# Attention and a feed-forward layer on one core: new figures for the SyncE queue, the loads and a chunk's pace in the table that orders the program

## The chip, the core and the metric

The kernel runs on 1 of the 8 cores of a Trainium2 chip. The metric is the device time of one execution in microseconds (us). Five instruction queues work side by side: TensorE (PE, with its weight loads listed as PEld), VectorE (DVE), ScalarE (ACT), GpSimd (POOL) and SyncE (SP). In this kernel SP issues nearly all DMA transfers. Each queue executes in its written order: an instruction whose input is late also holds everything behind it on its engine.

## The reference

Inputs are q, k and v of 8 batches, 8 heads, 576 positions and 64 dimensions in fp32. Per batch two attentions are added:

- **pooled**: q, k and v are averaged over groups of 4 positions (576 becomes 144), softmax attention runs over all 144, and each output row is repeated 4 times;
- **local**: each position attends to the positions less than 4 away.

The sum, as 8 x 576 = 4608 rows of 512, is the `x` of a feed-forward layer with a residual:

```python
mu = np.mean(x, axis=-1, keepdims=True)
var = np.mean((x - mu) ** 2, axis=-1, keepdims=True)
xn = (x - mu) / np.sqrt(var + 1e-06) * g_ln
ch = np.maximum(xn @ w_ch1, 0.0) @ w_ch2      # 512 -> 2048 -> 512
return (x + ch).astype(np.float32)
```

The two weight matrices arrive as 64-bit floats.

## The kernel before

**Work.** The 4608 rows are 36 tiles of 128 rows and 18 chunks of 256 rows. The feed-forward part runs per chunk over 8 pairs of 128 hidden columns. Each matrix product is done as three fp32r products of high and low parts: `up` (L996, 12 matmuls per 128 columns) makes `h`, ACT makes `hh` (L1003) and DVE its rest `hl` (L1007), and `down` (L1019, 6 matmuls) adds into `acc`. The local attention of a batch is cut into 5 windows of 116 rows, 40 windows in all (`local(i)`); the pooled attention goes by half batches (`pooled_half`). For each tile, `norm(n)` adds both attentions (`plus`, L896, POOL), takes mean and variance (`stats`, L904 to L907, DVE), scales (`normed`, L914, DVE, makes `xn`), transposes on PE (L923, makes `px`) and splits into `xh` (ACT, L930) and `xlo` (DVE, L940).

**Windows.** Windows 0 to 6 load q and k by rows (L428, tiles `qn`, `kn`) and transpose them on PE (L458, `lq`, `lk`); later ones load 32-wide blocks (L419, `qr`, `kr`) and transpose on DVE (L499, `lqt`, `lkt`). L437 and L443 load `vwin`. The exponentials are transposed on PE (L575) and copied by ACT (L582, `at`), multiplied with `vwin` on PE (L596, `lv`) and divided by DVE (L602 to L612) into `xl`. The rows of `xl` are moved by DMA from one SBUF place to another, into the tile `x` (L653 to L662); the first tiles are instead put together on PE (`expand`, L884 and L890, `ex`).

**Weights.** `weights(which, f)` is called 32 times, for 16 groups of 128 hidden columns of each matrix: two loads of 256 KB (L347 or L352, tile `s`), ACT takes the high word (L359, `cva`), DVE joins the low word (L367, L370), ACT makes the high part (L378, `hi`), and DVE or POOL the low part (L383, `lo`). All of this has to happen during about the first eighth of the run, while the first chunks already use the weights.

**What sets the order.** No instruction's place is written by hand. Every piece of work is a task: `add(engine, duration, function, dependencies, due, take, give, lag, ahead, alt, kb)`. `Plan.order` fills the engines' queues in a modelled time: among the tasks that can start soonest on an engine (within 0.5 us) it takes the one that is due first. `lag` is how long after its end a task's result can be used; for loads with `kb`, a running sum `moved` at `rate` KB per us puts the landing later when much is in flight. A load is not started more than `ahead` before its due time. `take` and `give` count rooms: 88 buffers of 2 KB per partition (`u`), which most tiles share, 8 PSUM banks (`a`) and 2 staging buffers (`stg`). A buffer that a window's `xl` held is given back when the last of its moves has landed. The due times follow the chunks: chunk c is due at 35 + 55 c, and the windows, the pooled halves and the weights are placed from that. The result is only an order; what waits for what on the chip is settled by semaphores. Where the plan sees PE idle in its first part, it lets PE multiply the identity matrix (L197), whose result nobody uses.

Of the kernel before, what the change touches and what calls it, by code (L numbers as in the profile page):

```python
# [22 lines left out]
class Plan:  # L23
# [3 lines left out]
    def __init__(self, rooms, spare):  # L27


        self.tasks = []  # L30
        self.rooms = rooms
        self.spare = spare
        self.cold = 3
        self.hold = 0.5
        self.lags = (80, 0.3, 0.6)
        self.rate, self.moved = 245.0, 0.0

    def add(self, eng, dur, fn, deps=(), due=0.0, take=(), give=(), lag=None, ahead=1e9, alt=None, kb=0):

        opts = {eng: (dur, fn, 0.0)}  # L40
        if alt is not None:
            opts[alt[0]] = alt[1:]
        t = SimpleNamespace(
            n=len(self.tasks), opts=opts, dur=dur, deps=[d for d in deps if d is not None],
            due=due, take=take, give=give, lag=lag, ahead=ahead, open=0.0, waits=0, eng=None, fn=None, kb=kb,
        )
        self.tasks.append(t)
        return t
# [91 lines left out]
def attention_then_ffn(  # L140
# [129 lines left out]

    T0 = 35
    C1 = 5
    CHUNK = 55
    PACE = CHUNK / NPR

    def chunk_at(c):
# [40 lines left out]
        return tuple(n.items())  # L317

    U, A, STG = (("u", 1),), (("a", 1),), (("stg", 1),)
    DMA, LAT, W_AHEAD = 0.5, 2.9, 40  # L320

    def act(n, sbuf=False):
        return (0.155 if sbuf else 0.14) + n / 1430.0
# [13 lines left out]
    def weights(which, f):  # L337
        key = (which, f)
        name = f"{which}_{f}"
        due = W0 + W_GAP * (f // 2) + 0.5 * (which - 1) + 1.0 * (f % 2)  # L340

        def load():
            x = box[key] = SimpleNamespace()
            x.raw = [unit([P, 512], f"s{name}_{i}", I32) for i in range(2)]
            for i in range(2):
                if which == 1:
                    nc.sync.dma_start(  # L347
                        x.raw[i].rearrange("p (c e) -> p c e", c=KC // 2),
                        w1[256 * i : 256 * (i + 1), f * 2 * P : (f + 1) * 2 * P].rearrange("(c p) e -> p c e", p=P),
                    )  # L350
                else:
                    nc.sync.dma_start(x.raw[i], w2[f * P : (f + 1) * P, 512 * i : 512 * (i + 1)])  # L352

        def high_word():

            x = box[key]
            x.a = unit([P, 512], f"cva{name}", I32)
            for i in range(2):
                nc.scalar.activation(  # L359
                    x.a[:, 256 * i : 256 * (i + 1)].bitcast(F32),  # L360
                    x.raw[i].rearrange("p (n two) -> p n two", two=2)[:, :, 1].bitcast(F32),
                    AF.Prelu, scale=REBIAS, alpha=-(2.0**32),
                )

        def low_word():
            x = box[key]
            nc.vector.tensor_single_scalar(out=x.a, in_=x.a, scalar=3, op=ALU.logical_shift_left)  # L367
            for i in range(2):
                a = x.a[:, 256 * i : 256 * (i + 1)]
                nc.vector.scalar_tensor_tensor(  # L370
                    out=a, in0=x.raw[i].rearrange("p (n two) -> p n two", two=2)[:, :, 0], scalar=29, in1=a,
                    op0=ALU.logical_shift_right, op1=ALU.bitwise_or,
                )

        def high():
            x = box[key]
            x.hi = unit([P, 512], f"hi{name}", F32R)
            nc.scalar.copy(x.hi, x.a.bitcast(F32))  # L378

        def low(eng):  # L380
            x = box[key]
            lo = unit([P, 512], f"lo{name}", F32R)
            eng.tensor_sub(lo, x.a.bitcast(F32), x.hi.bitcast(F32))  # L383
            weight[key] = (x.hi, lo)

        add = plan.add
        t = add("SP", 2 * DMA, load, (), due, take=(("u", 3),), lag=LAT, kb=512, ahead=W_AHEAD)
        t = add("ACT", 2 * act(256, True), high_word, (t,), due)
        t = add("DVE", 0.45 + 2 * dve(256), low_word, (t,), due, give=(("u", 2),))
        t = add("ACT", act(512, True), high, (t,), due, take=U)  # L390
        return add("DVE", dve(512), lambda: low(nc.vector), (t,), due, take=U, give=U,
                   alt=("POOL", pool(512), lambda: low(nc.gpsimd), 0.3))
# [12 lines left out]
    def local(i):  # L405
# [45 lines left out]
        for src, nm in ((q, "q"), (k, "k")):  # L451
            if by_pe:

                def turn(nm=nm):
                    p = psa(f"l{nm}{i}")
                    x.p[nm] = p
                    for pr in range(NPAIR):
                        nc.tensor.transpose(  # L458
                            p[:, pr * P : (pr + 1) * P],
                            x.raw[nm][:, 2 * pr : 2 * pr + 2].rearrange("p h d -> p (h d)"), ident,  # L460
                        )

                def turn_out(nm=nm):
                    t = unit([P, NPAIR, P], f"l{nm}t{i}")
                    nc.scalar.copy(t.rearrange("p c t -> p (c t)"), x.p[nm])
                    setattr(x, nm + "t", t)

                def sums(nm=nm):

                    for par in range(2):  # L470
                        t0 = window_start(w, par)
                        g0, g1 = (-(-(NQ * (2 * w + p)) // FACTOR) for p in (par, par + 1))
                        g1 = min(g1, SD)
                        c0 = 64 * par + FACTOR * g0 - t0
                        p = x.p[nm].rearrange("p (c t) -> p c t", c=NPAIR)
                        for hg in range(2):
                            key = (b, hg, nm)
                            if key not in gsum:
                                gsum[key] = unit([P, 2, SD], f"gs{nm}{b}_{hg}")
                            nc.vector.tensor_reduce(  # L480
                                out=gsum[key][:, :, g0:g1],
                                in_=p[:, 2 * hg : 2 * hg + 2, c0 : c0 + FACTOR * (g1 - g0)]
                                .rearrange("p c (g r) -> p c g r", r=FACTOR),
                                axis=AX.X, op=ALU.add,
                            )

                t = add("SP", 1.46, lambda src=src, nm=nm: load_rows(src, nm), (), due - 12.0, take=U,
                        lag=LAT, kb=256, ahead=AHEAD)
                t = add("PE", 0.43, turn, (t,), due - 8.0, take=A, give=U)
                if own:  # L490
                    t = add("DVE", 4 * dve(120), sums, [t] + gsum_done.get((b, nm), []), due - 8.0,
                            take=() if w else (("u", 2),))
                    gsum_done.setdefault((b, nm), []).append(t)
                turned.append(add("ACT", act(512), turn_out, (t,), due - 8.0, take=U, give=A))
            else:

                def turn(nm=nm):
                    t = unit([P, H, 64], f"l{nm}t{i}")
                    nc.vector.transpose(  # L499
                        t.rearrange("p h j -> p (h j)"), x.raw[nm].rearrange("p h j d -> p (h j d)")  # L500
                    )
                    setattr(x, nm + "t", t)

                ts = []
                for jb in range(2):
                    ts.append(add("SP", 4 * DMA, lambda src=src, nm=nm, jb=jb: load_blocks(src, nm, jb), ts,
                                  due - 14.0, take=() if jb else U, lag=LAT, kb=128, ahead=AHEAD))
                turned.append(add("DVE", dve(512), turn, ts, due - 8.0, take=U, give=U))
        vt = add("SP", 4 * DMA, load_v, (last_local.v[i % NVW],), due - 8.0, lag=LAT, kb=256, ahead=AHEAD)

        def scores_by_pair():

# [138 lines left out]
        for e, (n, p0, r0, m, par) in enumerate(moves):  # L651

            def move(n=n, p0=p0, r0=r0, m=m, par=par):  # L653
# [7 lines left out]
                for h2 in range(2):  # L661
# [2 lines left out]
                        x.xl[64 * h2 + r0 : 64 * h2 + r0 + m].rearrange("p (c n) d -> p n c d", n=2)[:, par],  # L664
                    )

            t = add("SP", DMA if by_pe else 2 * DMA, move, outs, due + 1.0, take=() if n in piece else U,
                    give=U if e == len(moves) - 1 else (), lag=LAT, kb=116)
            piece.setdefault(n, []).append(t)

# [11 lines left out]
    def pooled_half(b, hg):  # L682
# [8 lines left out]
        for nm, src in (("v", v),) if own else (("q", q), ("k", k), ("v", v)):  # L691
            for half in range(2):
# [21 lines left out]
                    eng.tensor_add(dst[:, half, :, :D], raw[:, :, :D], raw[:, :, D : 2 * D])  # L714

                by_dve = b == 0 and nm == "k"
                t = add("SP", 0.82, load, (), due - 4.0, take=STG, lag=LAT, kb=288, ahead=AHEAD)
                t = add(
                    "DVE" if by_dve else "POOL", dve(512) + dve(256) if by_dve else 2.1,
                    (lambda key=key: pool4(key, nc.vector)) if by_dve else pool4, [t, lastg.vd[hg] if nm == "v" else None] + ready.get(nm, []),  # L720
# [6 lines left out]
    def pooled_pair(b, hg, pr, x, ready):  # L727
# [119 lines left out]
        lastg.v = lastg.vd[hg] = t  # L847
        t = add("DVE", 0.68, divided, (t,), due, take=U if b < NPB and pr == 0 else (), give=A)
        od_done.append(t)
        t = add("SP", DMA, keep, (t,), due, lag=LAT)  # L850
        ud_done.setdefault(b, []).append(t)


# [2 lines left out]
    def norm(n):  # L856
# [103 lines left out]
                    piece.setdefault(n1, []).append(m1)  # L960
            kept = add("ACT", act(512), keep_x, (t,), due + 1.0, take=U)
        else:
            t = add("SP", DMA * len(rows), load_up, [d for _, _, b, _ in rows for d in ud_done[b]], due - 4.0,
                    take=U, lag=LAT, kb=256, ahead=12.0)
            t = add("POOL", pool(512), plus, [t] + piece[n], due - 3.0, give=U)
        t = add("DVE", 1.1, stats, (t,), due - 1.0)
# [149 lines left out]
```

## Time and profile before

| | before |
|---|---|
| median of 3 runs | 1068.04 us (1065.08 to 1068.09) |
| profiled execution, its own time | 1069.35 us |
| span of its instructions | 1067.0 us |
| PE busy | 1039.3 us, 97% |
| DVE busy | 509.5 us, 48% |
| ACT busy | 313.2 us, 29% |
| POOL busy | 268.7 us, 25% |
| granted TensorE clock | 0.990 in the mean |
| moved by DMA | 104.33 MB in 289,295 packets, 237,945 of them under 512 B |

The execution's own time is 2.35 us over its span. PE is busy nearly all the time, so its gaps are what can be lost or won; they are few, and they lie in the first 140 us and at two places later. In a list of waits, "A <- B" reads: A waited, and what came last was B. In a chain, each row is the work or the transfer that released the next. In the table by stages each engine's busy time is followed by its number of instructions, and the granted clock, the share of the DMA engines and GB/s stand at the end.

### The profile page before, as it was taken

The numbers are of one execution on the slowest core, as the hardware profiler recorded it, in microseconds if no ns is written. First come the engines' busy times: TensorE is split into PE (matmuls) and PEld (weight loads), VectorE is DVE, ScalarE is ACT, GpSimd is POOL, SyncE is SP. The second block draws the span as 40 slices with busy tenths as digits, with TensorE's granted clock in tenths as the row PEclk, the third lists the DMA queues.
The fourth block names the chain that finished last, engine by engine and source line by source line (L and its number), as shares of the span: only waits on it lengthen the run. The fifth ranks groups of instructions, "written<-read, shape, count | busy, mean of one in ns | idle before, by whom it ended". The sixth has DMA issues, their size and how long they took to land.

```text
span 1067.0 us, 23720 instructions
## 1 busy us (share of the span) xinstructions
PE 1039.3 (97%) x9280; PEld 932.2 (87%) x9280; DVE 509.5 (48%) x1307; ACT 313.2 (29%) x856; POOL 268.7 (25%) x286
## 2 busy tenths in 40 slices
PE   8897899989999999999999999999989999999998
PEld 8786789979999888889898989898989989888997
DVE  7589954634353534444444443545434454534211
ACT  5575632413332222132222221223222222222110
POOL 4233546323105221231224150142301400000000
PEclk9898999999999999999999999999999999999999
DMA  7788445535433533344354434243442443201000
GB/s 156 214 230 287 129 106 123 146 80 114 88 86 82 119 82 92 69 94 97 77 118 95 106 78 114 42 130 74 109 90 66 87 87 76 62 27 32 9 20 20
DMA packets 289295, 104.33 MB, mean 98 GB/s; under 512 B 237945, under 2 KB 276089, under 8 KB 289185
## 3 DMA queue, kind: packets, MB, share of 16 engines
q1 hardware_dynamic: 289185, 102.83, 40.7%
q8 instruction: 73, 1.20, 0.5%
q14 instruction: 37, 0.30, 0.1%
HBM read 82.58 MB, written 11.80 MB: 88 GB/s over the span
## 4 chain that ended last, share of the span: by engine, by line
PE 87%; DMA 4%; DVE 4%; SPq 2%; ACT 1%; issue 1%; POOL 0%; DVEq 0%; ACTq 0%; POOLq 0%
PE h L996 36%; PE acc L1019 35%; PE gv L802 3%; DMA s<-in_moe_w_ch_dram 3%; PE lv L596 2%; PE gs L766 2%; PE ls L540 2%; PE lt L575 1%; PE px L923 1%; PE gt L785 1%; SPq L428 1%; DVE cva L370 1%; DMA x<-xl 1%; PE gq L739 1%; DVE lo L383 1%
## 5 line engine op out<-in xcount | busy, mean ns | idle before, releaser
L1019 PE MATMUL acc<-hi,hl 128*128 128x512 f32 x576 | 238.2, 413 | 5.3 <-DVE hl L1007 5.3
L1019 PE MATMUL acc<-lo,hh 128*128 128x512 f32 x576 | 228.2, 396 | 0.0
L1019 PE MATMUL acc<-hi,hh 128*128 128x512 f32 x576 | 226.2, 393 | 0.0
L1003 ACT ACTIVATE hh<-h 128x512 fp32r<-128x512 f32 x144 | 86.2, 599 | 437.8 <-PE h L996 393.6
L1007 DVE SCALAR_TENSOR_TENSOR hl<-h,hh 128x512 fp32r<-128x512 f32 x144 | 98.9, 687 | 222.3 <-ACT hh L1003 214.7
L996 PE MATMUL h<-xh,lo 128*128 128x256 f32 x1152 | 193.2, 290 | 0.0
L996 PE MATMUL h<-xlo,hi 128*128 128x256 f32 x1152 | 185.3, 283 | 0.0
L996 PE MATMUL h<-xh,hi 128*128 128x256 f32 x1152 | 185.1, 283 | 0.0
L996 PEld LDWEIGHTS h<-xh,lo 128*128 128x128 f32 x1152 | 168.4, 190 | 16.9 <-POOL lo L383 0.2
L996 PEld LDWEIGHTS h<-xlo,hi 128*128 128x128 f32 x1152 | 159.1, 192 | 0.0
L996 PEld LDWEIGHTS h<-xh,hi 128*128 128x128 f32 x1152 | 158.6, 191 | 0.0
L896 POOL TENSOR_TENSOR x<-x,up 128x512 f32<-128x512 f32 x32 | 41.2, 1289 | 416.6 <-DMA x<-xl 310.9
L1019 PEld LDWEIGHTS acc<-hi,hh 128*128 128x128 f32 x576 | 109.0, 189 | 25.3
L1019 PEld LDWEIGHTS acc<-hi,hl 128*128 128x128 f32 x576 | 109.8, 191 | 22.0 <-DVE hl L1007 6.4
L1019 PEld LDWEIGHTS acc<-lo,hh 128*128 128x128 f32 x576 | 109.9, 191 | 12.5
L930 ACT ACTIVATE xh<-px,gain 128x128 fp32r<-128x128 f32 x144 | 43.6, 372 | 77.1 <-PE px L923 47.7
L940 DVE SCALAR_TENSOR_TENSOR xlo<-px,gain,xh 128x128 fp32r<-128x128 f32 x144 | 42.7, 344 | 34.7 <-ACT xh L930 34.5
L904 DVE BATCH_NORM_STATS2 st<-x 128x6 f32<-128x512 f32 x32 | 21.9, 686 | 47.1 <-POOL x L896 46.0
L779 ACT ACTIVATE ag<-gs,gmx 96x144 f32<-96x144 f32 x96 | 28.9, 373 | 42.9 <-DVE gmx L771 42.7
L1027 DVE SCALAR_TENSOR_TENSOR x<-acc,x 128x512 f32<-128x512 f32 x36 | 24.4, 688 | 35.3 <-PE acc L1019 35.3
L546 DVE TENSOR_TENSOR ls<-ls,mask 128x256 f32<-128x256 f32 x66 | 26.6, 424 | 27.2 <-PE ls L540 27.2
L802 PEld LDWEIGHTS gv<-vd,agt 72*72 72x72 f32 x512 | 37.2, 145 | 1.4
(191 smaller groups left out, 1156.8 us busy)
## 6 DMA issues: line engine op xcount, KB each, us to landing
s<-in_moe_w_ch_dram SPq DMA_DIRECT2D x64, 256.0 KB
vwin<-in_v_dram SPq DMA_DIRECT2D x160, 64.0 KB
out_dram<-x SPq DMA_DIRECT2D x36, 256.0 KB
qr<-in_q_dram SPq DMA_DIRECT2D x264, 32.0 KB
kr<-in_k_dram SPq DMA_DIRECT2D x264, 32.0 KB
up<-ud SPq DMA_DIRECT2D x28, 256.0 KB
x<-xl SPq DMA_DIRECT2D x66, 58.0 KB
ud<-od SPq DMA_DIRECT2D x32, 72.0 KB
```

Source lines behind the costliest of these rows:

```text
L546: nc.vector.tensor_add(x.ps[n], x.ps[n], mask.unsqueeze(1).broadcast_to([P, NPAIR, 64]))
L779: nc.scalar.activation(y.a[:, c], y.ps[:, c], AF.Exp, scale=POOLED_SCALE, bias=y.mx[:, c : c + 1])
L802: nc.tensor.matmul(y.pv[:, qh, h2], lhsT=y.at[kh][:, h2, qh * GH : (qh + 1) * GH], rhs=vd[:, kh, 2 * pr + h2], start=kh == 0, stop=kh == 1,)
L896: nc.gpsimd.tensor_add(xt[n], xt[n], x.up)
L904: nc.vector.bn_stats(st, x.up if by_pe else xt[n])
L930: nc.scalar.activation(xh[c][i][:, k, j * P : (j + 1) * P], pxt[n][:, kc], AF.Copy, scale=gain[:, kc : kc + 1])
L940: nc.vector.scalar_tensor_tensor(out=xlo[c][i][:, k, ts], in0=pxt[n][:, kc], scalar=gain[:, kc : kc + 1], in1=xh[c][i][:, k, ts].bitcast(F ...
L996: nc.tensor.matmul(ph[c, p][:, fi], lhsT=wt[:, kc], rhs=xx[kc // 2][:, kc % 2], start=n == 0, stop=n == 3 * KC - 1)
L1003: nc.scalar.activation(hh[c, p], ph[c, p], AF.Relu)
L1007: nc.vector.scalar_tensor_tensor(out=hl[c, p].rearrange("p c t -> p (c t)"), in0=ph[c, p].rearrange("p c t -> p (c t)"), scalar=0.0, in1=h ...
L1019: nc.tensor.matmul(acc[c][j], lhsT=lt[:, fi, ts], rhs=rt, start=p == 0 and fi == 0 and n == 0, stop=p == NPR - 1 and fi == 1 and n == 2,)
L1027: nc.vector.scalar_tensor_tensor(out=x, in0=acc[c][j], scalar=1.0 + 2.0**-23, in1=x, op0=ALU.mult, op1=ALU.add)
```

## The change

Only figures of the table change; no computation is added or removed.

- SP's time for issuing: a weight pair 1.3 (was 1.0), q or k by rows 1.33 (1.46), `vwin` 2.65 (2.0), a window's move 0.76 per DMA (0.5), a pooled load 0.45 (0.82), a pooled result 0.42 (0.5), the load of pooled rows for a tile 0.64 each (0.5).
- Landing: 2.5 after the issue for all loads (was 2.9), and 1.5 more, so 4.0, for weights.
- Weight on the transfers: 260 KB per us (was 245); q, k and v of windows count 360 or 200 KB (was 256 or 128).
- A chunk is due every 53 (was 55), and with it everything that is placed from the chunks.

```diff
-        self.rate, self.moved = 245.0, 0.0
+        self.rate, self.moved = 260.0, 0.0
...
-    CHUNK = 55
+    CHUNK = 53
...
-    DMA, LAT, W_AHEAD = 0.5, 2.9, 40
+    DMA, LAT, W_AHEAD, W_LAG = 0.5, 2.5, 40, 1.5
...
-        t = add("SP", 2 * DMA, load, (), due, take=(("u", 3),), lag=LAT, kb=512, ahead=W_AHEAD)
+        t = add("SP", 1.3, load, (), due, take=(("u", 3),), lag=LAT + W_LAG, kb=512, ahead=W_AHEAD)
...
-            t = add("SP", DMA if by_pe else 2 * DMA, move, outs, due + 1.0, take=() if n in piece else U,
+            t = add("SP", 0.76 if by_pe else 1.52, move, outs, due + 1.0, take=() if n in piece else U,
```

**Place 1: ACT, around the copy `at4` of window 4**, about 45 us after the start. `cva2_0<-s2_0` takes the high word of group 0 of the second matrix; it waits for that load. Before:

```order
L582 COPY at3_800<-lt3_784 128x512
L359 ACTIVATE cva2_0_819<-s2_0_0_754 128x256
L359 ACTIVATE cva2_0_819<-s2_0_1_755 128x256
L900 COPY x0_849<-ex0_793 128x512
L378 CAST hi1_0_856<-cva1_0_668 128x512
L582 COPY at4_868<-lt4_851 128x512
```

And with the change:

```order
L582 COPY at3_795<-lt3_778 128x512
L359 ACTIVATE cva1_1_806<-s1_1_0_597 128x256
L359 ACTIVATE cva1_1_806<-s1_1_1_598 128x256
L900 COPY x0_840<-ex0_787 128x512
L378 CAST hi1_0_851<-cva1_0_775 128x512
L582 COPY at4_863<-lt4_846 128x512
L359 ACTIVATE cva2_0_878<-s2_0_0_799 128x256
L359 ACTIVATE cva2_0_878<-s2_0_1_800 128x256
```

The weights' group 2_0 has moved behind `at4`; ahead of `at4` stands now group 1_1, which is loaded earlier.

**Place 2: PE, the transposes of window 6.** `lk6` is the transposed k of window 6, from the load `kn6`. Before, it stands between two halves of a `down` of the second pair, right ahead of the window's scores (L517, L526):

```order
L1019 MATMUL acc0_1_1253<-hi2_2_1369,hh0_1_1406 128x512
L458 MATMUL lk6_1483<-ident_66,kn6_976 128x128 x4
L1019 MATMUL acc0_0_1252<-hi2_3_1391,hl0_1_1417 128x512
L1019 MATMUL acc0_0_1252<-lo2_3_1408,hh0_1_1406 128x512
```

With the change it follows `lq6` right behind the first `up` of chunk 0 (`h0_0`), much earlier:

```order
L996 MATMUL h0_0_1081<-xlo0_0_968,hi1_1_1070 128x256 x2
L996 MATMUL h0_0_1081<-xlo0_1_980,hi1_1_1070 128x256 x2
L458 MATMUL lq6_1149<-ident_66,qn6_975 128x128 x4
L458 MATMUL lk6_1161<-ident_66,kn6_1013 128x128 x4
L197 MATMUL lt5_1168<-ident_66 128x128
L575 MATMUL lt5_1168<-ident_66,la5_1138 128x128 x4
```

On SP, meanwhile, `kn6` is still loaded at about the same place: behind the same q load, and now also behind the two moves into `x4`, but ahead of a weight pair that stood ahead of it.

**Place 3: DVE, tile 27**, about 790 us after the start. Before:

```order
L904 BN_STATS st27_10422<-x27_10140 128x6
L906 BN_AGGR mv27_10424<-st27_10422 128x2
L907 TENSOR_SCALAR mv27_10424<-mv27_10424 128x1
L499 STREAM_TRANSPOSE lqt33_10446<-qr33_10176 128x512
L499 STREAM_TRANSPOSE lkt33_10448<-kr33_10223 128x512
L914 TENSOR_SCALAR xn27_10465<-x27_10140,mv27_10424 128x512
```

With the change:

```order
L904 BN_STATS st27_10415<-x27_10126 128x6
L906 BN_AGGR mv27_10417<-st27_10415 128x2
L907 TENSOR_SCALAR mv27_10417<-mv27_10417 128x1
L1007 SCALAR_TENSOR_TENSOR hl12_6_10423<-h12_6_10355,hh12_6_10402 128x512
L940 SCALAR_TENSOR_TENSOR xlo13_0_10441<-px26_10404,gain_75,xh13_0_10420 128x128 x2
L914 TENSOR_SCALAR xn27_10451<-x27_10126,mv27_10417 128x512
L940 SCALAR_TENSOR_TENSOR xlo13_1_10453<-px26_10404,gain_75,xh13_1_10438 128x128 x2
L499 STREAM_TRANSPOSE lqt33_10484<-qr33_10192 128x512
```

The transpose `lqt33` has moved behind `xn27`. In the program before, the buffer that `lqt33` takes was that of window 31's `xl`; with the change that buffer goes to `xh13_1` (an ACT instruction of tile 26). Other buffers of `xl` are taken over sooner too, counted in matmuls that stand in PE's list between the last move out of `xl` and the new tile's first instruction: before, the four nearest are `hl7_2` (23, behind a store of `x`), `lqt24` (25), `lqt33` (25) and `lkt13` (26); with the change `hl13_3` (8), `xlo14_0` (12), `xlo9_0` (14), `xh13_1` (19) and `xh5_1` (20).

More of the change, by code (lines that the diff above doesn't have):

```diff
@@ L485, in sums @@
                             )
-                t = add("SP", 1.46, lambda src=src, nm=nm: load_rows(src, nm), (), due - 12.0, take=U,
-                        lag=LAT, kb=256, ahead=AHEAD)
+                t = add("SP", 1.33, lambda src=src, nm=nm: load_rows(src, nm), (), due - 12.0, take=U,
+                        lag=LAT, kb=360, ahead=AHEAD)
                 t = add("PE", 0.43, turn, (t,), due - 8.0, take=A, give=U)
@@ L506, in local @@
                     ts.append(add("SP", 4 * DMA, lambda src=src, nm=nm, jb=jb: load_blocks(src, nm, jb), ts,
-                                  due - 14.0, take=() if jb else U, lag=LAT, kb=128, ahead=AHEAD))
+                                  due - 14.0, take=() if jb else U, lag=LAT, kb=200, ahead=AHEAD))
                 turned.append(add("DVE", dve(512), turn, ts, due - 8.0, take=U, give=U))
-        vt = add("SP", 4 * DMA, load_v, (last_local.v[i % NVW],), due - 8.0, lag=LAT, kb=256, ahead=AHEAD)
+        vt = add("SP", 2.65, load_v, (last_local.v[i % NVW],), due - 8.0, lag=LAT, kb=360, ahead=AHEAD)
         def scores_by_pair():
@@ L716, in pooled_half @@
                 by_dve = b == 0 and nm == "k"
-                t = add("SP", 0.82, load, (), due - 4.0, take=STG, lag=LAT, kb=288, ahead=AHEAD)
+                t = add("SP", 0.45, load, (), due - 4.0, take=STG, lag=LAT, kb=288, ahead=AHEAD)
                 t = add(
@@ L849, in pooled_pair @@
         od_done.append(t)
-        t = add("SP", DMA, keep, (t,), due, lag=LAT)
+        t = add("SP", 0.42, keep, (t,), due, lag=LAT)
         ud_done.setdefault(b, []).append(t)
@@ L962, in norm @@
         else:
-            t = add("SP", DMA * len(rows), load_up, [d for _, _, b, _ in rows for d in ud_done[b]], due - 4.0,
+            t = add("SP", 0.64 * len(rows), load_up, [d for _, _, b, _ in rows for d in ud_done[b]], due - 4.0,
                     take=U, lag=LAT, kb=256, ahead=12.0)
```

## The prediction

> **What bounds the kernel now.** I read the page first, then PE by stages, then what PE waited for, and last the chain at the places found.
>
> ```profile
> span 1067.0 us, 23720 instructions
> PE 1039.3 (97%) x9280; PEld 932.2 (87%) x9280; DVE 509.5 (48%) x1307; ACT 313.2 (29%) x856; POOL 268.7 (25%) x286
> ```
>
> PE's own work is the bound: no edit of an order removes a matmul. What can move is the 27.7 us that PE is not busy (1067.0 - 1039.3) and what it does at a lowered clock. Where that lies, the stages show (span, busy time with the number of instructions per engine, then clock, DMA share, GB/s):
>
> ```profile
> 40.00:50.00 10.00, 6.80 (x86) 5.42 (x85) 5.50 (x20) 3.90 (x9) 2.39 (x3) 0.86 0.88 243
> 50.00:60.00 10.00, 10.00 (x49) 8.62 (x47) 5.20 (x14) 4.97 (x15) 1.09 (x2) 0.80 0.94 286
> ...
> 80.00:90.00 10.00, 6.91 (x44) 5.59 (x42) 9.86 (x17) 4.69 (x10) 4.53 (x5) 1.00 1.04 364
> 90.00:100.00 10.00, 7.77 (x63) 7.12 (x64) 7.91 (x16) 5.19 (x16) 3.05 (x3) 0.66 0.91 262
> 100.00:110.00 10.00, 8.59 (x86) 7.75 (x85) 9.76 (x23) 7.78 (x21) 4.86 (x4) 1.00 0.46 142
> 110.00:120.00 10.00, 8.59 (x56) 7.47 (x56) 9.86 (x19) 5.08 (x12) 3.98 (x4) 1.00 0.52 146
> 120.00:130.00 10.00, 8.05 (x52) 6.36 (x51) 9.86 (x15) 7.55 (x22) 7.28 (x6) 1.00 0.49 131
> 130.00:140.00 10.00, 8.03 (x54) 6.34 (x53) 8.57 (x16) 5.05 (x14) 4.91 (x5) 1.00 0.35 78
> 140.00:150.00 10.00, 10.00 (x82) 9.53 (x81) 6.75 (x17) 3.33 (x8) 2.55 (x3) 1.00 0.69 154
> 200.00:250.00 50.00, 46.97 (x400) 42.06 (x400) 18.45 (x49) 13.26 (x42) 15.32 (x16) 0.97 0.37 80
> 750.00:800.00 50.00, 47.23 (x429) 42.45 (x428) 21.29 (x55) 11.39 (x29) 10.46 (x11) 0.98 0.45 95
> ```
>
> Three things. From 80 to 140 PE lacks 12.1 us (60 less the six PE sums) while DVE is busy 9.8 of 10 in most stages: there DVE, which prepares weights, is the bound. Ahead of it, at 40 to 60, PE stands for 3.2 us and then runs at 0.80 to 0.86 of its clock. Later PE is full but for 3.0 us in 200 to 250 and 2.8 us in 750 to 800. The early stand, by the chain (start, length, what):
>
> ```profile
> 41.53 4.32 DMA s<-in_moe_w_ch_dram
> 45.87 0.43 ACT cva L359
> ...
> 47.29 0.50 ACT at L582
> ...
> 49.08 2.00 PE ex L884 x4
> 51.08 1.71 PE ex L890 x4
> 52.79 1.52 PE ex L884 x4
> 54.31 0.86 PE ex L890 x4
> ```
>
> ACT stands at a weight's load that lands at 45.85; `at4`, which PE needs next, is queued three instructions behind it. PE and DVE rows with their idle time in brackets show the price and who inherits it:
>
> ```profile
> 47.83 1.24 PE L596 MATMUL lv<-vwin,at 64*64 64x65 f32 x32 [3.20 <-ACT at L582]
> ...
> 56.75 1.03 PE L884 MATMUL ex<-xl,choice 128*128 128x256 f32 x4
> 57.61 0.60 PE L890 MATMUL ex<-od,spread 72*128 72x256 f32 x2
> ```
>
> ```profile
> 55.21 0.70 DVE L904 BATCH_NORM_STATS2 st<-ex 128x6 f32<-128x512 f32 x1 [3.91 <-PE ex L890]
> ```
>
> Four `ex` matmuls take 0.86 us at full clock (56.75 to 57.61); the sixteen from 49.08 to 55.17 took 6.09 instead of 3.44. So the stand costs 3.2 + 2.65 = 5.9 us, and DVE's full stretch starts that much late, at 55.21.
>
> **The change, part by part.** Nothing is added or removed, so every term is a wait that goes, shrinks or comes.
>
> A, the start. In the new order ACT's `cva2_0` stands behind `at4` (place 1), so the load no longer holds PE; what covers that load from there is PE's run of `ex` and the tiles' norm work. DVE would begin 5.9 us earlier. Not all of it can last. The weights must have landed, and from 80 to 100 the DMA share is 0.91 to 1.04, so they cannot land much earlier there; the chain in this stretch has loads of weights in it, and PE waits once more:
>
> ```profile
> 91.03 6.64 DMA s<-in_moe_w_ch_dram
> 97.73 5.36 DMA s<-in_moe_w_ch_dram
> ...
> 113.09 4.70 DMA s<-in_moe_w_ch_dram
> ```
>
> ```profile
> 92.23 1.13 PE L526 MATMUL ls<-lkt,lqt 64*64 64x64 f32 x32 [3.08 <-ACT lkt L465]
> ```
>
> The last row is another PE stand that the new order takes away, since `lk6` is transposed long before its scores (place 2). With DVE as the bound until 140, it is cover for DVE more than a gain of its own. Bounds: nothing, if the landings bind, to 5.9 + 3.1 = 9.0. I take **-4**, two thirds of the first price.
>
> B, the stand at 220, where the moves of window 8 stand late in SP's queue:
>
> ```profile
> 210.75 3.39 SPq L437 DMA_DIRECT2D vwin<-in_v_dram  x4
> ...
> 216.72 2.58 SPq L437 DMA_DIRECT2D vwin<-in_v_dram  x4
> ...
> 220.02 5.53 SPq L662 DMA_DIRECT2D x<-xl  x6
> 225.65 0.50 SPq L700 DMA_DIRECT2D raw6q<-in_q_dram  x1
> 226.24 1.08 SPq L700 DMA_DIRECT2D raw6k<-in_k_dram  x1
> ```
>
> ```profile
> 227.16 0.69 DVE L904 BATCH_NORM_STATS2 st<-x 128x6 f32<-128x512 f32 x1 [7.42 <-POOL x L896]
> ```
>
> Its price for PE is 3.0 idle + 0.03 x 50 = 1.5 of clock, 4.5. The old table gives a window's move 1.0 and `vwin` 2.0; the trace has 5.53 / 3 = 1.84 and 2.6 to 3.4. The new 1.52 and 2.65 are nearer, yet still short. In the new list one of the two `vwin` loads ahead of these moves is gone to an earlier place (2.6 to 3.4), but the two `raw6` loads have come in front (1.6). The balance, 1.0 to 1.8, is a fifth of DVE's 7.42. Bounds 0 to -4.5; I take **-1**.
>
> C, the stand at 790. DVE waits for a buffer that the last move out of window 31's `xl` sets free, and `xn27`, which PE needs, is behind it:
>
> ```profile
> 796.17 0.71 DVE L499 STREAM_TRANSPOSE lqt<-qr 128x512 f32<-128x512 f32 x1 [4.05 <-DMA x<-xl]
> 798.12 1.12 PE L923 MATMUL px<-ident,xn 128*128 128x128 f32 x4 [2.77 <-DVE xn L914]
> ```
>
> Price: 2.8 + 0.02 x 50 = 3.8. In the new order `xn27` is ahead of `lqt33` (place 3), and the buffer goes to `xh13_1` on ACT, behind which `px27` doesn't wait. Bounds 0 to -3.8; **-3**.
>
> D, new waits of that kind. With the change some buffers are taken over nearer behind a move (8 to 20 matmuls; before, 25 for the one that cost). What such waits cost so far, by the list of waits (total, times, longest):
>
> ```profile
> ACT hh L1003 <- DMA x<-xl: 13.2, 3, 5.4
> DVE lqt L499 <- DMA x<-xl: 8.4, 3, 4.0
> ```
>
> Six waits, 21.6 us on DVE and ACT, of which only the one at 790 opened a gap on PE: PE has other products of earlier chunks queued. Bounds: 0, to four new places at 3.8 each, 15. I take **+1**, near the five that cost nothing.
>
> Sum: -4 - 1 - 3 + 1 = **-7**. The profiled execution took 1069.35 (span 1067.0 and 2.35 around it), so 1062.35 for it; it lies 1.31 above the median of 1068.04, which gives **1061** for the median.
>
> TensorE's clock hangs on such gaps. The rows have 3.20 us of idle followed by a stage at 0.80, and 2.77 us in a stage of 0.98. The Trainium skill, "TensorE: Matmul & The Clock Gate", Part 1, says that after an idle window of about 3.4 us the clock is halved, and that it comes back after a window as long and busy. The trace agrees roughly: the stand of 3.20 us is followed by `ex` at half speed, the one of 2.77 us isn't. By that rule alone a new wait of 3.4 us, as in D, would cost about 1.7 us on top, as an estimate from its window; the sum would be about -5 with one such.
>
> **The rivals.**
>
> *Nothing moves (1068).* DVE's stretch to 140 is the bound, and it ends where the last weights land and are converted, the landings quoted above standing in the chain until 118; A is then waited out between 70 and 100, and B and C turn up one tile further, since SP is as full as before. For: DMA share 1.01 to 1.04 there, equal work. Against: at 100 to 140 the share is 0.35 to 0.52, so DVE alone binds there. Sum about 0 to -2.
>
> *All three stands go (1056).* A 5.9, B 3, C 3.8, no D: -12.7, so about 1055 to 1057. For: the three are single places, each with its instruction named. Against: B's queue is hardly lighter.
>
> *Slower, by the buffers (1074).* The mechanism of C at the new places: `xlo14_0` and `xlo9_0` stand on DVE right ahead of a tile's `xn`, `hl13_3` ahead of a `down`, `xh5_1` on ACT ahead of the splits. Each waits for a move's landing; at 3.8 each, three of them make +11.4 against A and B (-5): +6.4. It decides from the point where a landing, now modelled 0.4 us sooner (2.5, was 2.9), comes later than DVE's lead over PE. For: distances of 8 to 14 matmuls where 25 cost 2.8 us. Against: five waits of six were covered.
>
> *The move of `lk6` costs more than it gives.* PE now needs `kn6` behind the first `up`:
>
> ```profile
> 56.28 3.31 SPq L428 DMA_DIRECT2D kn<-in_k_dram  x2
> 62.18 1.72 SPq L956 DMA_DIRECT2D x<-xl  x2
> ```
>
> The two moves (1.72) now stand ahead of `kn6` and a weight pair (about 1.0) behind: issued by 59.6 + 0.7 = 60.3, landed 4.3 later (as the load at 41.53), 64.6. PE, 5.9 us ahead of its 65.7 at that `up`, comes there at 59.8: a stand of 4.8 us. DVE still has weights to join, so I count it as covered; if not, A is gone and the sum is -3 to 0. This is part of the first rival's chance.
>
> **How the numbers follow.** Mine, with one or two of the stands gone and 1057 to 1066 as its own range: 0.45. Nothing moves: 0.23. All three go: 0.13. Slower: 0.19. About 0.3%, 3.2 us, can be told from no change by a measurement of this kernel. Faster by more: 0.41 of my 0.45, all of the 0.13 and 0.03 of the second: 0.57. Slower by more: 0.17 of the last and 0.03 elsewhere: 0.20. The rest, 0.23, is no difference. The range holds the first three and the lower part of the last: 1053 to 1073.
>
> **What would show it.** A right: no PE wait on `at` near 45, clock 1.00 in 50 to 60, DVE's first `st` of tile 2 near 49 instead of 55.21, and PE full from about 136 instead of 140; wrong if PE stands at L458 near 60 and DVE's stretch still ends near 140. B: DVE's wait on POOL near 215 under 6 us. C: no PE wait on `xn` near 785. D: waits on "x<-xl" at L940, L930 and L1007 that open no PE gap. The forecast is wrong if PE's busy time plus waits past 150 grows by more than 4 us.

## The result, and the profile after

The changed kernel takes 1082.45 us in the median of 6 runs (1078.04 to 1086.01), the kernel before 1066.80 in its 6: a ratio of 1.0144, with a 95% interval of 1.0118 to 1.0170. It is slower by 15.7 us. The profiled execution took 1082.84. The page begins:

```profile
span 1080.9 us, 23774 instructions
PE 1040.3 (96%) x9290; PEld 933.6 (86%) x9290; DVE 511.9 (47%) x1309; ACT 312.7 (29%) x852; POOL 266.2 (25%) x285
```

PE's own work is what it was. Not busy are 40.6 us (1080.9 - 1040.3) instead of 27.7, so 12.9 of the 13.9 us of span are PE's gaps. The table by stages tells which part of the run. First the kernel before:

```profile
0.00:150.00 150.00, 131.86 (x1276) 115.46 (x1277) 120.29 (x299) 87.74 (x237) 58.52 (x73) 0.95 0.71 192
150.00:1050.00 900.00, 894.20 (x7935) 805.53 (x7934) 386.46 (x1004) 224.23 (x617) 210.22 (x214) 1.00 0.37 83
```

Then the changed one, with the later stages that lost most:

```profile
0.00:150.00 150.00, 132.79 (x1305) 118.39 (x1306) 120.83 (x297) 88.21 (x241) 60.24 (x76) 0.97 0.75 195
150.00:1050.00 900.00, 880.37 (x7828) 791.40 (x7827) 386.96 (x1006) 222.13 (x608) 205.93 (x210) 0.99 0.36 83
...
200.00:250.00 50.00, 45.01 (x410) 40.17 (x410) 19.37 (x55) 13.38 (x43) 13.55 (x14) 0.93 0.42 97
800.00:850.00 50.00, 44.22 (x375) 39.81 (x374) 20.53 (x53) 10.54 (x30) 11.63 (x12) 0.93 0.31 74
```

The first 150 us are a little better: 0.9 us less idle, and PE is busy at half its clock for 9.3 us (107.81 to 114.64, 128.29 to 131.71) instead of 12.3 (47.16 to 53.99, 91.54 to 98.37), which is worth 1.5. All that was lost, 13.8 us more of idle and some clock (0.99 where it was 1.00), lies behind them, where DVE, ACT and POOL do the same work as before and the DMA engines are no busier. What PE waited for, in the list of waits (total, times, longest):

```profile
PE px L923 <- DVE xn L914: 13.3, 6, 5.8
PE acc L1019 <- DVE hl L1007: 8.5, 5, 3.0
PE lt L575 <- ACT la L570: 6.1, 2, 5.0
```

The wait of `px` on `xn` was 2.8 us, once. Now it is 13.3, and all but 0.65 us of it in five places (PE's instructions, the idle time ahead of each in brackets):

```profile
303.42 0.66 PE L923 MATMUL px<-ident,xn 128*128 128x128 f32 x4 [2.77 <-DVE xn L914]
360.04 0.66 PE L923 MATMUL px<-ident,xn 128*128 128x128 f32 x4 [0.94 <-DVE xn L914]
583.18 0.66 PE L923 MATMUL px<-ident,xn 128*128 128x128 f32 x4 [1.98 <-DVE xn L914]
810.08 1.11 PE L923 MATMUL px<-ident,xn 128*128 128x128 f32 x4 [5.78 <-DVE xn L914]
868.83 0.66 PE L923 MATMUL px<-ident,xn 128*128 128x128 f32 x4 [1.21 <-DVE xn L914]
```

In the program these are tiles 9, 11, 19, 27 and 29, each the second tile of its chunk. In each case the tile ahead of it is being split, and one of its buffers is that of a window's `xl`: `xh4_1` that of `xl11`, `xh5_1` of `xl13`, `xlo9_0` of `xl22`, `xh13_1` of `xl31`, `xlo14_0` of `xl33`. At the largest, near 810, the queues of SP, ACT and DVE read:

```profile
793.03 2.06 SPq L419 DMA_DIRECT2D kr<-in_k_dram  x4
795.22 3.14 SPq L437 DMA_DIRECT2D vwin<-in_v_dram  x4
798.46 5.99 SPq L662 DMA_DIRECT2D x<-xl  x6
```

```profile
808.30 0.62 ACT L930 ACTIVATE xh<-px,gain 128x128 fp32r<-128x128 f32 x2 [8.93 <-DMA x<-xl]
```

```profile
790.16 0.73 DVE L612 TENSOR_TENSOR xl<-lv,lr 128x256 f32<-128x256 f32 x2
...
803.07 0.69 DVE L904 BATCH_NORM_STATS2 st<-x 128x6 f32<-128x512 f32 x1 [10.53 <-POOL x L896]
...
808.96 0.61 DVE L940 SCALAR_TENSOR_TENSOR xlo<-px,gain,xh 128x128 fp32r<-128x128 f32 x2 [4.17 <-ACT xh L930]
809.48 0.54 DVE L914 TENSOR_SCALAR xn<-x,mv 128x512 f32<-128x512 f32 x1
```

`xl31` is ready at 790.9. Its moves are issued from 798.46, since a `kr` and a `vwin` load (and two more) stand ahead of them on SP; the last is issued at 804.5, and ACT's `xh13_1`, which takes the buffer, starts at 808.30. DVE's `xlo13_0` waits for ACT, and `xn27` stands behind it in DVE's queue. So a late move stops the tile ahead, and through it the next. How far such moves lag I took from the trace for the 33 windows 7 to 39: from the end of `xl` to the start of its first move (nothing where the move goes at once), 0.9 us in the mean before, and 1.8 with the change (the longest 7.6, the one shown). Why, SP's queue near 290 shows; the kernel before:

```profile
285.77 0.51 SPq L700 DMA_DIRECT2D raw7q<-in_q_dram  x1
286.38 0.37 SPq L700 DMA_DIRECT2D raw7k<-in_k_dram  x1
286.83 6.26 SPq L662 DMA_DIRECT2D x<-xl  x6
293.15 3.49 SPq L437 DMA_DIRECT2D vwin<-in_v_dram  x4
```

and the changed one:

```profile
285.84 0.59 SPq L865 DMA_DIRECT2D up<-ud  x1
286.47 2.81 SPq L419 DMA_DIRECT2D kr<-in_k_dram  x4
289.33 2.64 SPq L437 DMA_DIRECT2D vwin<-in_v_dram  x4
292.07 5.90 SPq L662 DMA_DIRECT2D x<-xl  x6
```

The same `vwin` load stood behind the moves and stands now ahead of them.

### The profile page after: what moved, and what is told of

Same layout as the page of the kernel before. It is cut to its first block, busy times and chain, and to the rows that moved or that the text cites. A ratio compares the mean times of both kernels' runs of the same rounds, so it can differ in the third digit from the quotient of the medians.

```text
span 1080.9 us, 23774 instructions
## 1 busy us (share of the span) xinstructions
PE 1040.3 (96%) x9290; PEld 933.6 (86%) x9290; DVE 511.9 (47%) x1309; ACT 312.7 (29%) x852; POOL 266.2 (25%) x285
## 2 busy tenths in 40 slices
DMA packets 289296, 104.34 MB, mean 97 GB/s; under 512 B 237945, under 2 KB 276089, under 8 KB 289185
## 4 chain that ended last, share of the span: by engine, by line
PE 78%; DMA 9%; DVE 5%; SPq 4%; issue 2%; ACT 1%; POOL 1%; DVEq 0%; ACTq 0%; POOLq 0%
PE h L996 33%; PE acc L1019 32%; PE gv L802 3%; DMA s<-in_moe_w_ch_dram 2%; PE lv L596 2%; PE ls L540 2%; DMA x<-xl 2%; PE gs L766 2%; PE lt L575 1%; SPq L419 1%; PE px L923 1%; PE gt L785 1%; SPq L662 1%; DVE cva L370 1%; SPq L428 1%
## 5 line engine op out<-in xcount | busy, mean ns | idle before, releaser
L1019 PEld LDWEIGHTS acc<-hi,hl 128*128 128x128 f32 x576 | 110.1, 191 | 27.5 <-DVE hl L1007 11.4
```

The costliest lines, as they stand in the source:

```text
L1019: nc.tensor.matmul(acc[c][j], lhsT=lt[:, fi, ts], rhs=rt, start=p == 0 and fi == 0 and n == 0, stop=p == NPR - 1 and fi == 1 and n == 2,)
```

## The experiments

Three theories stood at the start. **P**: the pace of 53 alone makes the stands. **S**: the new issue times and landings make them. **R**: any reshuffling of so full an order costs some. "New" is the changed kernel, "old" the kernel before; diffs are against them.

**Pace or figures.** New with the old pace, and old with the new pace:

```diff
-    CHUNK = 53
+    CHUNK = 55
```

> The new table with one number put back: a chunk is due every 55 again. Theory P (the pace of 53 alone makes the stands, since all work runs far behind its due times and buffers that a move out of xl frees are taken over right behind it): PE's waits on xn near 303, 583, 810 and 868 are gone, PE waits past 150 sum to under 6 us (20 in the changed kernel), time 1062 to 1068. Theory S (SP's issue times and the shorter landing make them): waits stay, 1077 to 1084. Theory R (any reshuffling of so full an order costs some such stands): 1070 to 1077.

```diff
-    CHUNK = 55
+    CHUNK = 53
```

> The old table with only the pace changed, 53. Theory P: stands on xn at the places of the changed kernel (the buffers of xl13, xl22, xl31 and xl33 go to a splitting of a tile within 11 to 20 matmuls), 1076 to 1085. Theory S: none of them, 1064 to 1070. Theory R: 1070 to 1077.

Measured: 1064.12 (ratio 0.9987, 0.9970 to 1.0004) and 1086.90 (1.0196, 1.0148 to 1.0244). P holds (the second is 2 us above its range), S falls: one number carries the whole loss, and more. With 55 the new figures can't be told from the old ones. PE's waits on `xn`, first in new with 55, then in old with 53:

```profile
PE px L923 <- DVE xn L914: 5.7, 2, 3.4
```

```profile
PE px L923 <- DVE xn L914: 15.0, 4, 7.5
```

With 53 they lie at 307, 587, 817 and 877, the same tiles. With 55 one of 3.4 near 797 is left, the old stand C, so "under 6 us past 150" was too hopeful (8.9 with the wait on `la` near 233 and one of 1.1). Moves follow `xl` after 0.8 us with 55, after 1.7 with 53.

**Tell the plan that moves land later.** The pace stays 53:

```diff
-                    give=U if e == len(moves) - 1 else (), lag=LAT, kb=116)
+                    give=U if e == len(moves) - 1 else (), lag=5.0, kb=116)
```

> The changed kernel, but the plan is told that a move out of xl lands 5.0 us after its issue (2.5 in the changed table); the pace stays 53. If the stands come from moves that land later than planned, they go although the pace stays: PE's waits past 150 under 8 us, 1066 to 1072. If the pace does harm in another way (loads that crowd SP, transfers), it stays at 1078 to 1084.

1083.27 (1.0158, 1.0125 to 1.0191): nothing gained. The splittings take the buffers later now (`xh4_1` 30 matmuls behind, `xlo13_0` 40 instead of `xh13_1` 19), and PE still stands on `xn` for 10.8 us at 305, 589 and 814. SP near the last:

```profile
791.90 2.67 SPq L437 DMA_DIRECT2D vwin<-in_v_dram  x4
794.61 2.64 SPq L419 DMA_DIRECT2D qr<-in_q_dram  x4
...
800.37 2.64 SPq L437 DMA_DIRECT2D vwin<-in_v_dram  x4
803.10 5.95 SPq L662 DMA_DIRECT2D x<-xl  x6
```

`xl` was ready at 794.7, and 8 us of loads stood ahead of its moves. So here it isn't the landing that the plan has wrong, but the queue ahead of the issue. That became theory **Q**: loads ahead of the moves in SP's queue.

How the pace gets into this queue can be read from SP's list of instructions and from its waits. PE of the kernel before takes 55.1 us per chunk (the first `px` of tile 4 comes at 186.22, that of tile 26 at 791.94), so a plan with 53 gets 2 us further ahead of PE in each chunk. There are four `vwin` buffers, taken in turn: the load for window w + 4 overwrites what `lv` of window w reads, and `xl` of window w is made from that `lv`. With 53 this load stands ahead of the moves out of that `xl` in 16 of the 33 windows (17 in old with 53, 5 in new with 54, none in the kernel before and in new with 55, 56 or 57). There SP can be held up by PE. In SP's list of waits of the changed kernel:

```profile
SPq L437 <- PE lv L596: 22.4, 9, 5.9
```

In old with 53 this is 32.6 us in 11 waits, with 54 it is 7.4 in 3, and in the kernel before and with 55, 56 and 57 there is no such row. Of the five stands on `xn`, those at 583, 810 and 869 have such a load ahead of their moves, and at 583 and 869 SP waits there; those at 303 and 360 have not.

**Other paces.** New with 57, 54 and 56 (one line each, like this):

```diff
-    CHUNK = 53
+    CHUNK = 57
```

> The new table with a chunk due every 57, slower than PE's real pace. Theory P: no stand on xn, as with 55, 1061 to 1068. If the plan only fits when due times and PE's pace agree, loads and windows come late and it loses, 1072 or more. Theory R: 1070 to 1077.

> The new table with a pace of 54. In this order no splitting of a tile (xh, xlo) takes a buffer of xl within 34 matmuls of its last move. Theory F (only such places cost): no stand on xn over 2 us but at lqt35, 1062 to 1069. Theory P as a trend (each us of pace below PE's own costs): 1070 to 1076, between 55 and 53.

> The new table with a pace of 56. Here xh5_0 and xh14_0 take buffers of xl13 and xl33 within 24 matmuls. Theory F: stands on xn at those two places, near 360 and 865, of 1 to 4 us each, and 1065 to 1072. Theory P as a trend, with 57 at 1076 and 55 at 1064: 1067 to 1073, with the loss in the first 150 us and not at those two places.

Measured: 1076.09 (1.0100, 1.0071 to 1.0129), 1070.22 (1.0036, 1.0020 to 1.0051) and 1064.45 (0.9982, 0.9967 to 0.9996). From 53 to 56 the row 1082, 1070, 1064, 1064 is a trend; R, by which any reshuffling costs, doesn't fit 55 and 56. At 54 no splitting took a buffer nearby and yet it loses, in many waits of 0.5 to 3.1 us, so near buffers (F) are not the whole: moves lag 1.3 us there. At 56 both places of F were right, 346 and 849.6, with 0.2 and 0.6 us only, and the largest stand, 2.6 near 791, wasn't among them. Moves lag 1.2 us there, nearly as long as with 54, and it costs nothing: the mean alone isn't the price. 57 missed what P expected: it stands on `hl` (6.5 us) and `ktg` (4.4), with none over 2.1 on `xn`. From 50 to 100 PE works 39.7 us, where 55 has 41.9, but at a clock of 0.96 instead of 0.90, so this stretch doesn't hold the 12 us. A pace can be too slow too; I did not follow that.

**Take load off SP's queue, all other orders unchanged.** New, 53, without 33 `vwin` loads:

```diff
-                    for h2 in range(2):
+                    for h2 in range(0):
```

> The changed kernel without the vwin loads of windows 7 to 39: SP doesn't issue them (the windows use what the buffer held, so this part of the local attention isn't computed from its own v); every other engine's order is the same word for word, and so is SP's without them. If moves come late because loads that take longer than planned stand ahead of them in SP's queue, the moves now follow xl at once (1.8 us behind it in the mean of the changed kernel, up to 7.6), and PE's stands on xn (12.7 us) fall to under 4: 1064 to 1071. If the 4 to 5 us from a move's issue to its landing are enough for the stands by themselves, more than half of them stays: 1075 to 1082.

1061.50 (0.9961, 0.9946 to 0.9976): 21 us less, with the pace of 53 and the orders of PE, DVE, ACT and POOL word for word. No wait on `xn` past 150 is left. SP and the stages:

```profile
776.52 2.06 SPq L419 DMA_DIRECT2D kr<-in_k_dram  x4
778.68 5.91 SPq L662 DMA_DIRECT2D x<-xl  x6
```

```profile
150.00:1050.00 900.00, 896.62 (x7963) 807.14 (x7962) 386.76 (x1010) 225.22 (x613) 205.33 (x210) 1.00 0.32 74
```

PE's idle time past 150 falls from 19.6 to 3.4 us. Moves follow `xl` after 0.5 us. Buffers of `xl` still go to `xh5_1`, `xh9_1` and `xh14_1` 20 matmuls behind a move: a near buffer costs nothing if the move is in time. Two things changed besides the queue. Some buffers are taken over a little later (those of `xl22`, `xl33` and `xl31` after 20, 20 and 28 matmuls instead of 14, 12 and 19; `xh5_1` keeps its 20). And 4 x 64 KB per window aren't moved, so this run alone can't divide queue from traffic; the runs with POOL below, which move the same bytes, do.

**Put load on SP's queue at the old pace.** Old, with the 33 loads issued twice:

```diff
-                    for h2 in range(2):
+                    for h2 in (0, 1, 0, 1):
```

> The kernel before, but each vwin load of windows 7 to 39 is issued twice (the same bytes to the same place; all other orders are the same word for word). SP has 2.6 to 3.5 us more to issue per window. Theory Q (loads ahead of the moves in SP's queue make the stands, not the pace as such): stands on xn appear with the old pace of 55, moves follow xl 2 us and more later in the mean (0.9 before), 1074 to 1095. If the pace harms by other ways (buffers, transfers): the transfers have room at a share of about 0.4, and it stays within 1065 to 1069.

1183.82 (1.1092, 1.1051 to 1.1134). The direction of Q, far beyond its range: moves follow `xl` after 4.0 us, 16 of 33 after more than 4. PE's waits, SP's, and one of the loads:

```profile
PE px L923 <- DVE xn L914: 36.8, 6, 8.0
PE lt L575 <- ACT la L570: 13.2, 1, 13.2
```

```profile
SPq L437 <- DMA vwin<-in_v_dram: 99.2, 72, 4.0
```

```profile
221.48 7.96 SPq L437 DMA_DIRECT2D vwin<-in_v_dram  x8
```

The edit did more than it was meant to. The second copy of a load writes the same place as the first, and SP waits until the first has landed: 72 waits, 99.2 us. Issuing itself is no dearer, 0.60 us each in the median (0.62 before). So a window got 5 us, not 3, and half of that is waiting. Nor is all of the loss the stands on `xn`: past 150 PE stands for 90 us, 36.8 of them on `xn`, the others on `la`, `ktg`, `kd` and more, which I did not follow back.

**Issue these loads elsewhere.** Nothing is left out; the plan puts them on POOL, in new with 53 and with 55, and on ACT with 55:

```diff
-                        nc.sync.dma_start(
+                        nc.gpsimd.dma_start(
...
-        vt = add("SP", 2.65, load_v, (last_local.v[i % NVW],), due - 8.0, lag=LAT, kb=360, ahead=AHEAD)
+        vt = add("SP" if by_pe else "POOL", 2.65, load_v, (last_local.v[i % NVW],), due - 8.0, lag=LAT, kb=360, ahead=AHEAD)
```

> The changed kernel, pace 53, with the vwin loads of windows 7 to 39 issued by POOL and not by SP, nothing left out. Theory Q: SP is relieved of 2.65 us per window as without these loads, no stand on xn over 2 us, 1060 to 1066. If POOL's issuing holds up its own sums (plus) as much as SP's held the moves: 1070 and more.

> The same with a pace of 55. Theory Q: SP has room at both paces, so pace hardly matters now: within 3 us of the run with 53, 1058 to 1064. If pace acts beside SP's queue, this is 5 us and more below the run with 53.

> The new table, pace 55, with these loads issued by ACT. ACT is 29% busy and has 85 us more to issue; theory Q: 1058 to 1065. If an issuing of 2.65 us in ACT's queue makes hh late: PE's waits on hl grow over 10 us in sum and it takes 1070 and more.

Measured: 1075.86 (1.0077, 1.0050 to 1.0103) with 53; **1056.12** (0.9907, 0.9876 to 0.9939) with 55, which beats both kernels; 1069.96 (1.0037, 1.0023 to 1.0050) on ACT. The one with 55 on POOL, by stages:

```profile
0.00:200.00 200.00, 186.66 (x1795) 167.94 (x1796) 150.45 (x370) 107.05 (x300) 100.17 (x120) 0.97 0.71 183
200.00:1050.00 850.00, 848.47 (x7521) 763.84 (x7520) 356.81 (x939) 204.70 (x552) 248.20 (x298) 1.00 0.35 79
```

and with 53:

```profile
0.00:200.00 200.00, 179.08 (x1649) 160.40 (x1650) 144.25 (x352) 103.23 (x284) 91.95 (x114) 0.93 0.67 171
200.00:1050.00 850.00, 845.25 (x7522) 760.17 (x7522) 361.38 (x952) 210.09 (x573) 255.23 (x304) 1.00 0.36 82
```

Past 200, PE's idle time is 1.5 and 4.8 us, with the same bytes moved as in the kernels before (104.34 MB, though in 257,616 packets instead of 289,296): Q holds there for both paces, but for a stand of 2.5 us on `xn` that is left with 53, near 806. But 53 still loses 7.6 us of PE's work and 0.04 of the clock in the first 200 us, so my "pace hardly matters now" was wrong: what 53 costs is not SP's queue alone. It is not the pace alone either: the changed kernel, also with 53, has 180.83 us of PE's work at a clock of 0.97 in its first 200.

The time with 53 lies in the range of the other answer, that POOL's issuing holds up its own sums. POOL's waits with 53 say that it is held up, by the same wait as SP:

```profile
POOL vwin L437 <- PE lv L596: 121.1, 15, 17.9
```

With 55 these are 27.5 us in 3 waits, and DVE's waits for `plus` are 22.8 us instead of 66.6. But the waits come almost all behind 200, where PE loses only 4.8 us; they are not where the 20 us between the two runs lie. POOL issues a `vwin` load in 0.62 us (as SP does), about 2.5 for the four. ACT is not the place: not `hl`, as I had expected, but its own `agt` and `la` come late (4.2 and 3.6 us of PE's waits).

**True times for SP instead of relief.** New with 55:

```diff
-                    ts.append(add("SP", 4 * DMA, lambda src=src, nm=nm, jb=jb: load_blocks(src, nm, jb), ts,
+                    ts.append(add("SP", 2.24, lambda src=src, nm=nm, jb=jb: load_blocks(src, nm, jb), ts,
...
-        vt = add("SP", 2.65, load_v, (last_local.v[i % NVW],), due - 8.0, lag=LAT, kb=360, ahead=AHEAD)
+        vt = add("SP", 2.9, load_v, (last_local.v[i % NVW],), due - 8.0, lag=LAT, kb=360, ahead=AHEAD)
...
-            t = add("SP", 0.76 if by_pe else 1.52, move, outs, due + 1.0, take=() if n in piece else U,
+            t = add("SP", 0.76 if by_pe else 1.98, move, outs, due + 1.0, take=() if n in piece else U,
```

> The new table at a pace of 55 with SP's times nearer to the trace: q and k blocks 2.24 (2.0), vwin 2.9 (2.65), a window's move 1.98 (1.52). No splitting takes a buffer of xl within 30 matmuls, and lqt33 doesn't take that of xl31. If SP's queue is the weak point of the plan, the stand near 797 (3.4 in the new table with 55) goes and the one near 233 shrinks: 1058 to 1063. If not: 1063 to 1068.

1065.18 (0.9984, 0.9972 to 0.9997): the stand near 233 went, the one near 796 stayed at 2.8. Better figures for the queue hardly help; less in the queue does.

**What is left of the pace, and what the new figures are worth.** Old with the loads on POOL, at 55 and at 53, and new at 56, all with the first line below; the second is the old table's, and `CHUNK` is set as said:

```diff
-                        nc.sync.dma_start(
+                        nc.gpsimd.dma_start(
...
-        vt = add("SP", 4 * DMA, load_v, (last_local.v[i % NVW],), due - 8.0, lag=LAT, kb=256, ahead=AHEAD)
+        vt = add("SP" if by_pe else "POOL", 4 * DMA if by_pe else 2.65, load_v, (last_local.v[i % NVW],), due - 8.0, lag=LAT, kb=256, ahead=AHEAD)
```

> The old table, pace 55, with the vwin loads of windows 7 to 39 issued by POOL. If the new figures gain 2 to 4 us in the first 150 us (term A), this is 2 to 5 us above the run with the new table (1056.1): 1058 to 1061, with the stand on at near 48. If the figures gain nothing and only the queue counts: 1054 to 1058.

> The old table with a pace of 53 and the relief. If the rest of the loss (20 us between 53 and 55 with SP relieved) belongs to the pace alone: 1072 to 1082. If it comes from the pace together with the new figures: 1056 to 1066.

> The new table with 56 and the relief. If only a pace below PE's own harms: within 3 us of 55, 1054 to 1060, no stand on xn. If 55 is just a lucky order: 1062 or more.

Measured: 1058.08 (0.9925, 0.9901 to 0.9948), 1068.49 (1.0023, 1.0004 to 1.0042), 1059.25 (0.9935, 0.9915 to 0.9956). In the first PE doesn't stand once past 150 (900.00 us of 900), and its stand on `at` near 47 is still there (3.1 us). 56 comes within about 3 us of 55, so 55 is not a lucky order. With SP relieved, 53 costs 10 us in the old table, between the two answers that I had allowed, and 20 in the new. In the new table it lies mostly ahead of 200 us (stages above); what carries it there is open.

## Why the prediction was wrong

- **The forecast** (1061, faster) failed; what came is the rival "slower, by the buffers", to which I gave 0.19. Its mechanism is in the trace word for word, at three of the places named (`xh5_1`, `xlo9_0`, `xlo14_0`) and at two others; the fourth, `hl13_3`, the nearest of all, cost PE nothing. Its price, 1074, was 8 us short.
- **A (-4)**: right in kind, a little over half the size in this kernel (0.9 of idle and 1.5 of clock up to 150). `at4` no longer holds PE, and the clock is 1.00 from 50 to 60. Tile 0's `px` starts 6.5 us earlier (48.48 instead of 55.01):

```profile
48.48 0.60 PE L923 MATMUL px<-ident,xn 128*128 128x128 f32 x4
...
62.08 0.66 PE L458 MATMUL lk<-ident,kn 128*128 128x128 f32 x4 [1.42 <-DMA kn<-in_k_dram]
```

  At tile 4 (186.22 before, 184.08 now) 2.1 are left; PE also stands for 2.0 near 179, first on `agt`, which is in none of my terms. The stand on `kn6` came, with 1.4 us where I had worked out 4.8. Where SP is relieved, the new figures at 55 end 4.7 us ahead of the old ones by the two profiled spans (1052.6 and 1057.3), 2.0 by the medians; the intervals of the two (0.9876 to 0.9939, 0.9901 to 0.9948) overlap, so this gain isn't shown.
- **B (-1)**: wrong sign. I counted which loads stood ahead of the moves and found 1.0 to 1.8 us less; but the moves began only 0.5 earlier (219.49, not 220.02) and took 7.9 us to issue, not 5.5 (why, isn't shown), and PE's wait went from 3.0 to 5.0, with a clock of 0.93 where it was 0.97:

```profile
219.49 7.91 SPq L662 DMA_DIRECT2D x<-xl  x6
```

- **C (-3)**: the step that failed is "the buffer goes to `xh13_1` on ACT, behind which `px27` doesn't wait". `px27` waits for `xn27`, that stands in DVE's queue behind `xlo13_0`, and `xlo13_0` waits for ACT. I had quoted both rows in the order (place 3) and followed only one queue. The stand grew from 2.8 to 5.8.
- **D (+1)**: the step that failed is "near the five that cost nothing". I had counted how near a buffer is taken over, in matmuls, and took the moves to be as punctual as before. They were not. The four stands other than C's make 6.9 us. With D, B and C the idle time is accounted for: 6.9 + 2.0 + 3.0 and the 2.0 near 179, less 0.9 at the start, is 13.0 of 12.9 us.
- **What I had not asked**: which part of the table moves loads past the moves. I weighed SP's figures, edit by edit, and gave the pace no term at all. In the order of SP's queue at each window it could have been seen: the 16 `vwin` loads that stand ahead of the moves only with the new pace.
- **The clock**: I misread the stand of 2.77 us. It was followed by half speed: its row in the prediction has 1.12 us for four `px`, where the one at 303.42 has 0.66, behind a stand just as long. So the length alone doesn't decide. The granted clock, where PE goes on behind the stand of 2.77 in the kernel before, and then behind those of 5.0 and 5.8 in the changed one:

```profile
798.12:801.60 3.48, 3.48 (x13) 3.09 (x14) 2.24 (x7) 2.91 (x11) 0.00 (x0) 0.51 0.25 78
```

```profile
235.36:241.00 5.64, 5.64 (x20) 4.87 (x20) 1.79 (x3) 2.21 (x8) 0.00 (x0) 0.51 0.27 41
810.08:815.00 4.92, 4.92 (x18) 4.20 (x19) 3.49 (x9) 2.44 (x8) 0.00 (x0) 0.56 0.21 32
```

  That is 1.7 us before, where I had priced 1.0 in C, and 2.8 and 2.2 now. By the Trainium skill, "TensorE: Matmul & The Clock Gate", Part 1, each would cost some 1.7 us, as I estimated from it. The trace agrees for the first; for the two long ones the measurement is 1.1 and 0.5 more, and it decides. The stages of 50 us have 0.07 x 50 = 3.5 for each, too much: the clock fell while PE still stood, where it costs nothing.

## What to carry to other kernels

An engine that only issues transfers is a queue like any other: what stands ahead of the transfer that something waits for counts in full, at 0.3 to 1 us for each, and so does any wait of that queue for a buffer. When a change of a planner's figures reshuffles a program, compare that queue around the late transfers first, then follow each wait through every in-order queue that it blocks. If it is too full, take work out of it: moving a sixth of its issuing (84 of 514 us between 200 and 900) to an idler engine gained more than any better figure.

## What the runs showed that I had not expected

One number that only sets due times, 4% off, cost 1.7 to 2% of the time. SP's queue had so little room that 33 extra groups of loads, with SP's waits for their landing, cost the kernel before 118 us, while leaving out the same groups gained the changed one 21. And POOL, whose sums the tiles wait for, could issue 132 loads, with a pace of 55, at no cost that shows past 200: the Trainium skill, "DMA: Bandwidth & Descriptors", "Issuing engines are not separate DMA queues", says that several issuing engines save only the sequencer's time for issuing, "usually small relative to the DMA itself". The trace agrees on what is saved, and here it was not small: 2.65 us per window.
